# The front of a banded-attention and feed-forward kernel, planned by another rule for the port that VectorE and GpSimd share, with the weight casts on other engines

## The chip, the cores and the metric

The kernel runs on one core of a Trainium2 chip. The metric is the device time of one execution in microseconds (us), as the median of several executions. In the text PE or TensorE is the matrix engine, DVE is VectorE, ACT is ScalarE, POOL is GpSimd and SP is SyncE, which issues nearly all DMAs of this kernel.

## What is computed

Eight batches of eight heads with 576 positions of 64 elements go through attention within a window of 32 positions to either side. The result, read as 4608 tokens of 512 elements, goes through two matrix products with a squared ReLU between them:

```python
scores = scale * np.matmul(q, k.transpose(0, 1, 3, 2))
mask = np.abs(pos[:, None] - pos[None, :]) <= window          # window = 32
scores = np.where(mask, scores, -1000000000.0)
attn = np.exp(scores - np.max(scores, axis=-1, keepdims=True))
attn = attn / (np.sum(attn, axis=-1, keepdims=True) + 1e-09)
x = np.matmul(attn, v)            # then turned into (4608, 512)
...
h = x @ w_in                      # (4608, 512) @ (512, 2048)
r = np.maximum(h, 0.0)
g = s * (r * r) + b
return (g @ w_out).astype(np.float32)   # (4608, 2048) @ (2048, 512)
```

All inputs and the output are float32; the kernel computes its matrix products in bf16.

## The kernel before

The tokens are cut into 36 attention tiles of 128 (index `j`). Tiles 0 and 1 take a short way (`attend_light`): their scores are computed twice, plain and transposed, so that no transposition of the exponentials is needed. Their maxima are taken by DVE, split into two bf16 parts (`M16`, lines 861 and 863), turned on PE (`flip`, line 819), copied (`MT`), subtracted on PE (`less`, line 824), and ACT takes the exponential. Then come the product with V (`av`, lines 833 to 840), the division (`XN`, line 892), a turn back on PE (line 900) and a copy into `XT`, from which the feed-forward part reads. The other tiles go through `attend`: scores on PE (line 938), mask and maximum on DVE (line 950), exponential on ACT (line 958), the sum's reciprocal on DVE (line 967), the division of P (line 972), a transposition of P by PE (line 995, tiles below 5) or by DMA (line 986), and the product with V (line 1017 below tile 8, lines 1034 and 1040 from there on).

K and Q of the first 576 positions come in by four raw loads, `K0`, `K1`, `Q0` and `Q1`, one half of the heads each. They are cast to bf16 in pieces (`FLAT`), turned by PE (line 679) and copied into `TURN`. Tiles 0 to 3 read those. Later K and Q come in row order (`r32k`, `r32q`), are cast (`KQN`) and are turned by PE (line 756) or, above tile 11, by DMA.

The feed-forward part works on tiles of tokens, `TILES`, 8 of 128 and then 14 of 256. For each it multiplies by `WIN` in groups of 16 matmuls (8 of twice the width in a wide tile; line 1170), ACT applies the ReLU (line 1179), DVE squares into `GT` (line 1198), and PE multiplies `GT` by `WOUT`, in four parts of four matmuls, one part for each quarter of `w_out` (line 1220). The first scale and bias come in through `cvec` and `spread_scalars`: DVE splits `s` and `b` into three bf16 parts (lines 1087 and 1090), PE spreads them over the partitions.

`w_in` and `w_out` are loaded as float32 in four quarters each (`i0` to `i3`, `o0` to `o3`; line 584) into staging slots (`SLOT`), which lie in parts of `GT` that are not in use yet, and in the output buffers (slot 4). Each quarter is cast to bf16 by four casts (`cast`, through `move`, whose DVE and POOL form is line 633 and whose ACT form is line 638). `WSET` names the engines that may do that.

The order of the instructions on every engine is fixed when the program is built, by the planner `_Plan`. Each operation is a node with a key, an engine or a tuple of engines to choose from, a cost in ns for each, and what it reads and writes. `order` goes through time: it takes the engine that is free first, and there the ready node with the lowest key. With a choice of engines, a node is left to another engine if it would end sooner there. Every engine then runs its list in that order, and semaphores hold an instruction until what it needs is done; nothing else orders the engines. Where PE stands idle in the plan, `fill` writes in matmuls on constants (lines 555 and 559). `FIRST` gives the order of the first loads on SP's queue, `LEAD`, `L0` and `LS` by how many tokens attention's keys run ahead of those of the feed-forward part (`akey`), `RELU`, `AVK`, `HC`, `HT_`, `CB`, `SKEY` and others shift the keys of single operations, and `HOLD` is by how much a key may be higher for PE to stay with small matmuls. `CSET` names the engines for the casts of K and Q, `FLEX` those for the copies of turned K and Q, `NDIV` the tiles below which DVE may divide P, `NSQ` those in which POOL may square.

Of the kernel before, what the change touches and what calls it, by code (L numbers as in the profile page):

```python
# [11 lines left out]
S = 576  # L12
# [14 lines left out]
HOLD, DEFER, CHANGE = 200.0, 200.0, 97.0  # L27
LOOK, LOOK_GAP, LOOK_END = 0.0, 0.0, 400000.0
WARM, WARM_LOW, WARM_OVER, WARM_NS, WINDOW, WARM_END = 1.0, 0.66, 0.0, 225.0, 3413.0, 28000.0
BANKS_ = (("HT", 1), ("HT", 0), "AV", "TP")  # L30
FILL, FILL_MIN, FILL_SHARE, FILL_NS = ("attn", "sums"), 400.0, 0.5, 220.0


class _Node:
# [4 lines left out]
                 "hard", "mode", "ahead", "end")  # L39

    def __init__(self, nid, eng, fn, cost, lat, key, dsem, ndma, dtime):
        self.nid = nid
        self.eng = eng
        self.fn = fn
        self.cost = cost
        self.lat = lat
        self.key = key
        self.deps = {}
        self.dsem = dsem
        self.ndma = ndma  # L50
        self.dtime = dtime
# [11 lines left out]
        self.mode = "full"  # L63
        self.ahead = ()
        self.end = None
# [24 lines left out]
class _Plan:  # L90
# [11 lines left out]
    def add(self, eng, fn, cost, key, reads=(), writes=(), dsem=None, ndma=1, dtime=0.0,  # L102
# [3 lines left out]
        n.ndesc = ndesc  # L106

# [40 lines left out]
    def order(self):  # L148
# [5 lines left out]
        free = {e: START for e in self.ENGS}  # L154
        done = []
# [26 lines left out]
        while len(out) < len(self.nodes):  # L182
# [39 lines left out]
            if isinstance(n.eng, tuple):  # L222
                for x in n.eng:
                    cand[x].remove(n)
                n.eng, n.cost, n.fn = e, n.cost[e], n.fn[e]
            else:
                cand[e].remove(n)
            out.append(n)
# [132 lines left out]
def bass_sliding_window_symmetric__then__act_starrelu_kernel(  # L361
# [13 lines left out]
    TILES = [128] * 8 + [256] * 14  # L375
    assert sum(TILES) == T
    LEAD, L0, LS = 560, 600, 70
    NSQ = 8
    RELU, SQ = 900, 200
    FIRST = "Q0 K0 Q1 K1 i0 v0 v1 i1 i2|v2 i3 k2 o0 v3 q4 q5 v4 o1 o2 o3||v5||"  # L380
    ANY = ("act", "dve", "pool")
    WSET = {"i": ("pool", "act", "dve"), "o": ("act", "pool", "dve")}
    VOP = 12
    HSTEP, CB, VOK = 1.5, -400, -100
    NFLEX, TAIL = 10, 2
    PDMA, KQDMA, AHEAD, GATE = 5, 11, 4, 5
    CKEY, SKEY = 100, -300
    SLOT = dict(i0=0, i1=1, i2=2, i3=3, o0=0, o1=1, o2=4, o3=2)
    RAWNS, NSPLIT = 1450, 1
    HC, HT_ = -500, 150  # L390
    WHOLE, LIGHT, CH, NDIV = 4, 2, S // 16, 2
# [5 lines left out]
    AVK, NOLD, ONE, NVO, DA = 384, 8, 11, 2, 2  # L397
# [5 lines left out]
    def CSET(j):  # L403
        return ("pool",) if j >= 8 else ("pool", "act")
# [7 lines left out]
    with ExitStack() as es:  # L412
# [672 lines left out]
        def spread_scalars(x1):  # L1085
            for i in range(3):
                add("dve", lambda e, i=i: e.tensor_copy(SC3[:, i, :], SC1[:, i, :]), 100, SKEY,
                    reads=["SC1"], writes=[("SC3", i)], after=[x1])
                if i < 2:
                    add("dve", lambda e, i=i: e.tensor_tensor(  # L1090
                        SC1[:, i + 1, :], SC1[:, i, :], SC3[:, i, :], ALU.subtract), 100, SKEY,
                        reads=["SC1", ("SC3", i)], writes=["SC1"])

            def spread_sc(e):
                for i in range(3):
                    r = e.matmul(TPF[:, 0:2], lhsT=ONES[0:1, 0:128], rhs=SC3[:, i, :], start=(i == 0),
                                 stop=(i == 2))
                return r

            add("pe", spread_sc, 200, SKEY, reads=["ONES"] + [("SC3", i) for i in range(3)], writes=["TP"])  # L1100
# [15 lines left out]
        def attention_until(n):  # L1116
            if n and done[0] == 0:
                loads(0)
            for j in range(done[0], n):
# [13 lines left out]
                if j == 1:  # L1133
                    spread_scalars(lastx[0])
# [166 lines left out]
```

## Time and profile before

| what | value |
|---|---|
| median of 3 runs | 317.06 us (316.82 to 317.52) |
| the profiled execution's own time | 316.83 us |
| its span, first to last instruction | 315.1 us |
| PE busy | 302.9 us, 96% of the span |
| DVE busy | 226.0 us, 72% |
| ACT busy | 229.6 us, 73% |
| POOL busy | 149.6 us, 47% |
| granted TensorE clock | 1.000 |

The span is what lies between the first and the last instruction; the rest of the time lies around it. Busy shares are means over the whole span, so that a stretch of 20 us in which another engine is full can't be seen in them: it takes the view of busy time by windows, and the timeline of the engine in question. In a timeline row stand start and length in us, the engine, the line, the operation, what is written and read, the shapes, the count, and in brackets the idle time before it and what ended that. A few per cent of the matmul records are missing, and a missing one shows as idle time of PE.

### The profile page before, as it was taken

What the parts mean: (1) busy time and instruction counts of PE and PEld (TensorE: products, weight loads), DVE (VectorE), ACT (ScalarE), POOL (GpSimd) and SP (SyncE); (2) the same over time, 40 slices, a digit from 0 to 9 for tenths busy, and PEclk for the clock granted to TensorE, in tenths of its full rate; (3) what the DMA queues carried; (4) which work ended last, traced back from release to release, by engine and by line L of the source; (5) the groups of instructions that cost most, each with busy time, mean ns of one, the idle gap of its engine ahead of it and who ended that gap; (6) DMA issues with size and microseconds to landing.
All of it is one profiled execution on the core that took longest, in us unless ns stands there. A gap on an engine that the chain in (4) does not pass through costs nothing.

```text
span 315.1 us, 10310 instructions
## 1 busy us (share of the span) xinstructions
PE 302.9 (96%) x4006; PEld 210.6 (67%) x4054; DVE 226.0 (72%) x915; ACT 229.6 (73%) x763; POOL 149.6 (47%) x195
## 2 busy tenths in 40 slices
PE   7998989999999999999999999999999999999996
PEld 3567757677776666677676666666766666676574
DVE  5779998978887867587787677767776766773343
ACT  6559767898678969597879687868787787873240
POOL 5435555377564746646454545554564555130000
PEclk9999999999999999999999999999999999999999
DMA  7999999899999999999999999799999872432101
GB/s 289 351 342 244 292 301 215 232 155 210 211 209 222 199 209 225 228 213 174 228 239 178 182 215 260 159 233 175 249 177 251 145 162 68 69 69 67 69 34 69
DMA packets 156070, 61.57 MB, mean 195 GB/s; under 512 B 130164, under 2 KB 146932, under 8 KB 156020
## 3 DMA queue, kind: packets, MB, share of 16 engines
q1 hardware_dynamic: 156016, 60.90, 94.5%
q8 instruction: 32, 0.52, 0.7%
q14 instruction: 18, 0.15, 0.2%
q10 hardware_dynamic: 4, 0.00, 0.0%
HBM read 37.03 MB, written 9.44 MB: 147 GB/s over the span
## 4 chain that ended last, share of the span: by engine, by line
PE 88%; DVE 6%; issue 2%; DMA 2%; POOL 1%; SPq 0%; ACT 0%
PE ht L1170 37%; PE outp L1220 19%; PE ptp L1220 18%; PE sc L938 4%; DMA gt<-in_q_dram 2%; PE tp L1034 1%; PE av L1040 1%; DVE gt L1198 1%; PE sc L1220 1%; DVE ss L950 1%; PE tp L756 1%; POOL p L972 1%; DVE outs L1234 1%; PE ht L679 1%; DVE vo L633 1%
## 5 line engine op out<-in xcount | busy, mean ns | idle before, releaser
L1170 PE MATMUL ht<-xt,win 128*128 128x256 bf16 (+1 forms) x1408 | 146.4, 253 | 1.1 <-issue 1.0
L1170 PEld LDWEIGHTS ht<-xt,win 128*128 128x128 bf16 x1408 | 116.4, 98 | 32.1 <-issue 1.1
L958 ACT ACTIVATE p<-ss,mx 128x128 bf16<-128x128 f32 x272 | 113.4, 420 | 7.7 <-DVE mx L950 7.0
L1179 ACT ACTIVATE r<-ht 128x512 bf16<-128x512 f32 x144 | 84.6, 587 | 46.4 <-PE ht L1170 45.1
L1198 DVE TENSOR_TENSOR gt<-r 128x512 bf16<-128x512 bf16 x144 | 80.6, 560 | 48.3 <-ACT r L1179 46.5
L972 POOL TENSOR_TENSOR p<-p,rc 128x512 bf16<-128x512 bf16 x68 | 75.6, 1132 | 80.3 <-DVE rc L967 79.1
L1220 PE MATMUL outp<-wout,gt 128*128 128x512 bf16 (+1 forms) x263 | 68.0, 373 | 3.0 <-issue 1.5
L950 DVE CUSTOM_DVE_ANT_0 ss<-sc,mask 128x128 f32<-128x128 f32 x272 | 64.6, 280 | 7.8 <-PE sc L938 7.8
L1220 PE MATMUL ptp<-wout,gt 128*128 128x512 bf16 x251 | 65.0, 379 | 2.2 <-issue 1.6
L958 ACT ACTIVATION_READ_ACCUMULATOR p<-ss,mx 128x1 f32 x272 | 52.0, 191 | 0.0
L1220 PEld LDWEIGHTS outp<-wout,gt 128*128 128x128 bf16 x288 | 27.0, 98 | 19.6 <-issue 0.9
L1220 PEld LDWEIGHTS ptp<-wout,gt 128*128 128x128 bf16 x272 | 25.3, 98 | 21.2
L633 POOL CAST ve<-v 128x512 bf16<-128x512 f32 x37 | 23.8, 647 | 21.2 <-PE av L1040 19.4
L1049 ACT COPY half<-tp 128x512 f32<-128x512 f32 x28 | 16.4, 584 | 14.1 <-PE av L1040 13.8
L633 POOL CAST kn<-r32k 128x512 bf16<-128x512 f32 x31 | 19.8, 664 | 9.9 <-DMA r32k<-in_k_dram 9.8
L1051 DVE TENSOR_TENSOR xt<-av,half 128x512 bf16<-128x512 f32 x28 | 19.1, 682 | 4.5 <-ACT half L1049 4.4
L633 POOL CAST qn<-r32q 128x512 bf16<-128x512 f32 x30 | 20.0, 668 | 4.7 <-DMA r32q<-in_q_dram 4.7
L950 DVE DVE_READ_ACCUMULATOR2_ANT mx<- 128x1 f32 x272 | 21.4, 79 | 0.0
L938 PEld LDWEIGHTS sc<-kt,qt 64*64 64x64 bf16 x768 | 10.8, 108 | 8.9 <-issue 7.8
L964 DVE TENSOR_SCALAR sm<-sm 128x8 f32<-128x8 f32 x34 | 6.3, 184 | 12.5 <-ACT p L958 12.5
L938 PE MATMUL sc<-kt,qt 64*64 64x64 bf16 (+1 forms) x768 | 14.3, 204 | 0.0
L1234 DVE SCALAR_TENSOR_TENSOR outs<-outp,scb,cvec 128x512 f32<-128x512 f32 (+1 forms) x18 | 13.1, 726 | 1.1 <-PE outp L1220 0.9
(165 smaller groups left out, 220.0 us busy)
## 6 DMA issues: line engine op xcount, KB each, us to landing
out_dram<-outs SPq DMA_DIRECT2D x35, 256.0 KB, 3.1
v<-in_v_dram SPq DMA_DIRECT2D x28, 256.0 KB, 5.4
r32q<-in_q_dram SPq DMA_DIRECT2D x28, 256.0 KB, 4.6
r32k<-in_k_dram SPq DMA_DIRECT2D x9, 512.0 KB, 5.4
gt<-in_moe_w_in_dram SPq DMA_DIRECT2D x4, 1024.0 KB, 10.1
gt<-in_moe_w_out_dram SPq DMA_DIRECT2D x3, 1024.0 KB, 9.9
v<-in_v_dram SPq DMA_DIRECT2D x8, 192.0 KB, 4.7
r32k<-in_k_dram SPq DMA_DIRECT2D x3, 448.0 KB, 4.6
```

The costliest lines, as they stand in the source:

```text
L633: return e.tensor_copy(dst, src)
L938: r = e.matmul(SC[hh][64 * u:64 * u + 64, pr, x0:x1], lhsT=qq, rhs=kk, start=True, stop=True)
L950: lambda e, ss=ss, x=x, y=y, pr=pr, hh=hh: e.tensor_tensor_reduce(out=SS[ss][:, x, :], in0=SC[hh][:, pr, :], in1=MASK[kind][:, :], scale=- ...
L958: lambda e, ss=ss, x=x, y=y: e.activation(P[pb][:, y, :].rearrange("q (a p t) -> q a p t", a=2, t=2), spread(SS[ss][:, x, :]), AF.Exp, bia ...
L972: return e.tensor_tensor(P[pb][:, y0:y0 + 4, :], P[pb][:, y0:y0 + 4, :], RC[mb][:, y0:y0 + 4].unsqueeze(2).broadcast_to([128, 4, 128]), AL ...
L1049: add("act", lambda e: e.copy(HALF[hb][:, :], AV2[:, :]), 482, key + AVK, reads=[AV2N], writes=[("HALF", hb)])
L1051: add("dve", lambda e: e.tensor_tensor(XT[:, :, 128 * (j % NX):128 * (j % NX) + 128], AV[:, :, :], HALF[hb][:, :].rearrange("p (a b) -> p ...
L1170: r = e.matmul(hbank[:, nt * f:nt * f + nt], lhsT=WIN[:, kc, 128 * ft:128 * ft + 128], rhs=XT[:, kc, x0:x0 + nt], start=(kc == 0), stop=(k ...
L1179: return e.activation(R1[rb][:, :], hbank[:, :], AF.Relu, bias=0.0, scale=1.0)
L1198: return e.tensor_tensor(d, r, r, ALU.mult)
L1220: r = e.matmul(op_[:, 0:cn], lhsT=GT[:, g_, fc, :], rhs=WOUT[:, fc, c0:c0 + cn], start=(fc == 0), stop=(fc == 15))
L1234: add("dve", lambda e, ob=ob, op_=op_, c0=c0, cn=cn: e.scalar_tensor_tensor(OUTS[ob][:, 0:cn], op_[:, 0:cn], SCB[:, 0:1], CVEC[:, c0:c0 + cn],
```

## The change

The planner gets a rule for the port that DVE and POOL share. Every node that writes one of the named tensors (`SHARED`) is marked. When a POOL node, or a marked DVE node, is placed before 70 us of planned time, its cost is made longer by what the other engine's last such node still has to run, less 100 ns (DVE) or 140 ns (POOL). The rule acts in the planner's reckoning only: no instruction and no semaphore is added for it.

Beside it the parameters are set anew. `w_in`'s 16 casts may be done by POOL alone, `w_out`'s 16 by ACT or POOL, none by DVE. `FIRST` loads both halves of Q ahead of K, `q4` and `v3` ahead of `o0`, and `k2` behind it; the staging slots of `o1`, `o2` and `o3` change, so that `o3` now waits for `o0`'s casts. K and Q casts are for any engine below tile 4 and for POOL from there on. DVE may divide P below tile 6. ScalarE may copy turned K and Q below tile 4 only. The splitting of the scalars becomes a function of its own with an early key, ahead of all attention. Ten tiles of 128 tokens stand in front, and 13 of 256 behind them. `HOLD` is doubled, and the keys of attention's first tiles, of the ReLU and of the product with V move.

```diff
-HOLD, DEFER, CHANGE = 200.0, 200.0, 97.0
-LOOK, LOOK_GAP, LOOK_END = 0.0, 0.0, 400000.0
+HOLD, DEFER, CHANGE = 400.0, 200.0, 97.0
+LOOK, LOOK_GAP, LOOK_END = 0.0, 50.0, 400000.0
+HELD, HELD_END = {"dve": 100.0, "pool": 140.0}, 70000.0
+SHARED = ("FLAT", "WIN", "WOUT", "VE", "VO", "KQN", "GT", "M16", "SC1", "SC3")
...
+        if writes:
+            n.shared = (writes[0][0] if isinstance(writes[0], tuple) else writes[0]) in SHARED
...
+            n.base = n.cost
+            if (e == "pool" or e == "dve" and n.shared) and t < HELD_END:
+                n.cost += max(0.0, held["dve" if e == "pool" else "pool"] - t - HELD[e])
+                held[e] = t + n.cost
...
-    TILES = [128] * 8 + [256] * 14
+    TILES = [128] * 10 + [256] * 13
-    LEAD, L0, LS = 560, 600, 70
-    NSQ = 8
-    RELU, SQ = 900, 200
-    FIRST = "Q0 K0 Q1 K1 i0 v0 v1 i1 i2|v2 i3 k2 o0 v3 q4 q5 v4 o1 o2 o3||v5||"
+    LEAD, L0, LS = 560, 470, 40
+    NSQ = 0
+    RELU, SQ = 700, 200
+    FIRST = "Q0 Q1 K0 K1 i0 v0 v1 i1 i2 v2 i3 q4 v3 o0|k2 q5 v4 o1 o2 o3 v5||||"
-    WSET = {"i": ("pool", "act", "dve"), "o": ("act", "pool", "dve")}
-    VOP = 12
+    WSET = {"i": ("pool",), "o": ("act", "pool")}
+    VOP = 8
-    NFLEX, TAIL = 10, 2
+    NFLEX, TAIL = 4, 2
-    CKEY, SKEY = 100, -300
-    SLOT = dict(i0=0, i1=1, i2=2, i3=3, o0=0, o1=1, o2=4, o3=2)
+    CKEY, SKEY = 100, -9350
+    SPLIT1, SPKEY = True, -9000
+    SLOT = dict(i0=0, i1=1, i2=2, i3=3, o0=0, o1=4, o2=1, o3=0)
-    HC, HT_ = -500, 150
-    WHOLE, LIGHT, CH, NDIV = 4, 2, S // 16, 2
+    HC, HT_ = -9500, -50
+    WHOLE, LIGHT, CH, NDIV = 4, 2, S // 16, 6
-    AVK, NOLD, ONE, NVO, DA = 384, 8, 11, 2, 2
+    AVK, NOLD, ONE, NVO, DA = 320, 8, 11, 2, 2
-        return ("pool",) if j >= 8 else ("pool", "act")
+        return ("pool",) if j >= 4 else ANY
...
-        def spread_scalars(x1):
+        def split_scalars():
             for i in range(3):
-                add("dve", lambda e, i=i: e.tensor_copy(SC3[:, i, :], SC1[:, i, :]), 100, SKEY,
-                    reads=["SC1"], writes=[("SC3", i)], after=[x1])
+                add("dve", lambda e, i=i: e.tensor_copy(SC3[:, i, :], SC1[:, i, :]), 100, SPKEY,
+                    reads=["SC1"], writes=[("SC3", i)], after=[lastx[0]] if lastx[0] else [])
...
+        def spread_scalars():
             def spread_sc(e):
...
                 loads(0)
+                if SPLIT1:
+                    split_scalars()
...
-                    spread_scalars(lastx[0])
+                    if not SPLIT1:
+                        split_scalars()
+                    spread_scalars()
```

More of the change, by code (lines that the diff above doesn't have):

```diff
@@ L38 @@
                  "nout", "left", "ready", "users", "seq", "used", "val", "snap", "pre", "tag", "ndesc",
-                 "hard", "mode", "ahead", "end")
+                 "hard", "mode", "ahead", "end", "shared", "base")
     def __init__(self, nid, eng, fn, cost, lat, key, dsem, ndma, dtime):
@@ L63, in __init__ @@
         self.mode = "full"
+        self.shared = False
+        self.base = 0.0
         self.ahead = ()
@@ L154, in order @@
         free = {e: START for e in self.ENGS}
+        held = {"dve": 0.0, "pool": 0.0}
         done = []
@@ L1083, in cvec @@
                 reads=["TP", "SCB"], writes=["CVEC"])
-        def spread_scalars(x1):
+        def split_scalars():
             for i in range(3):
-                add("dve", lambda e, i=i: e.tensor_copy(SC3[:, i, :], SC1[:, i, :]), 100, SKEY,
-                    reads=["SC1"], writes=[("SC3", i)], after=[x1])
+                add("dve", lambda e, i=i: e.tensor_copy(SC3[:, i, :], SC1[:, i, :]), 100, SPKEY,
+                    reads=["SC1"], writes=[("SC3", i)], after=[lastx[0]] if lastx[0] else [])
                 if i < 2:
                     add("dve", lambda e, i=i: e.tensor_tensor(
-                        SC1[:, i + 1, :], SC1[:, i, :], SC3[:, i, :], ALU.subtract), 100, SKEY,
+                        SC1[:, i + 1, :], SC1[:, i, :], SC3[:, i, :], ALU.subtract), 100, SPKEY,
                         reads=["SC1", ("SC3", i)], writes=["SC1"])
+        def spread_scalars():
             def spread_sc(e):
@@ L1098, in spread_sc @@
                 return r
-            add("pe", spread_sc, 200, SKEY, reads=["ONES"] + [("SC3", i) for i in range(3)], writes=["TP"])
+            add("pe", spread_sc, 200, SKEY, reads=["ONES"] + [("SC3", i) for i in range(3)],
+                writes=["TP"])
             add("act", lambda e: e.copy(SCB[:, :], TPF[:, 0:2]), 250, SKEY, reads=["TP"], writes=["SCB"])
```

## The prediction

> **What bounds the kernel now.** I read the busy table of the page first, then busy time by windows, then the chain of waits between 23 and 45 us, then the timelines of DVE, POOL and PE there. All numbers are of the profiled execution (316.83 us, span 315.1). The windows, with engines in the order PE, weight load, DVE, ACT, POOL:
>
> ```profile
> core 0: us, PE busy (x) PEld busy (x) DVE busy (x) ACT busy (x) POOL busy (x), PEclk, DMA share, GB/s
> 5.00:23.00 18.00, 17.23 (x338) 10.44 (x338) 13.32 (x36) 10.28 (x24) 7.23 (x12) 1.00 1.09 360
> 23.00:45.00 22.00, 18.92 (x337) 15.74 (x340) 21.73 (x83) 17.00 (x56) 13.07 (x16) 1.00 1.03 285
> 45.00:70.00 25.00, 24.31 (x338) 17.03 (x341) 21.36 (x87) 21.40 (x75) 13.55 (x18) 1.00 1.03 198
> 70.00:300.00 230.00, 226.57 (x2894) 156.82 (x2933) 162.21 (x687) 174.47 (x599) 112.29 (x137) 1.00 0.99 182
> ```
>
> From 70 us on PE is full and DVE is at 70%: what comes after the front is matrix work that this change leaves as it is. Between 45 and 70 us PE lacks 0.69 us. The one stretch in which PE is not full and another engine is, is 23 to 45 us: DVE 21.73 of 22.00, PE 18.92, so 3.08 us without a PE record. (Part of that is missing records.) Between 5 and 23 us PE is busy 17.23 of 18.00, but the matmuls on constants that the planner writes into its idle time (line 555) are in it:
>
> ```profile
> 5.00:23.00 18.00, 4.28 (x14) 1.02 (x14) 1.00 1.09 360
> ```
>
> So 4.28 us of that stretch is filling. Reclaimable in the front are 4.28 + 0.77 (5 to 23 us), 3.08 and 0.69: under 8.9 us. The first 5 us belong to the first loads and don't change. The chain of waits (start, length, what) says who is responsible behind 24.9 us:
>
> ```profile
> 25.94 0.33 DVE xn L892
> 26.27 0.75 DVE win L633 x2
> ...
> 28.62 0.08 DVE sc L1087
> 28.70 0.19 DVE ss L950
> 28.89 0.01 DVE mx L950
> 28.89 0.07 DVE sc L1090
> 28.97 0.17 DVE sm L964
> 29.13 0.06 DVE sc L1087
> 29.19 0.18 DVE rc L967
> 29.37 0.01 DVE sc L1090
> ...
> 29.59 0.93 DVE sc L1087
> ...
> 32.03 0.06 DVE wout L633
> 32.09 0.61 issue
> 32.70 0.75 DVE wout L633 x2
> ...
> 38.27 2.63 POOL p L972 x2
> ...
> 40.95 0.62 PE av L995 x8
> ```
>
> The chain runs through DVE until 38.2 us, then through two divisions of P on POOL, and reaches PE only at 40.95.
>
> **What the change takes off that chain.** The rows just shown give the terms. `w_in`'s two casts: 0.75 us, gone from DVE. `w_out`'s three casts with the gap between them: 0.06 + 0.61 + 0.75 = 1.42 us, gone from DVE. The five scalar operations: 0.08 + 0.07 + 0.06 + 0.01 + 0.93 = 1.15 us, moved ahead of attention. Together 3.32 us. The 0.93 is a cast of two numbers; the next rows show why it took so long:
>
> ```profile
> 29.52 1.00 DVE L1087 CAST sc<-sc 1x2 bf16<-1x2 f32 x1
> ```
>
> ```profile
> 29.46 1.04 POOL L972 TENSOR_TENSOR p<-p,rc 128x512 bf16<-128x512 bf16 x1 [1.17 <-DVE sc L1090]
> ```
>
> It ended (30.52) with POOL's division (30.50). That is the shared port, which the old planner did not reckon with, and it also stretches the squares and casts beside POOL work. By engine, from 11.7 to 48.4 us (count, busy us, mean ns), DVE first, then POOL and ACT:
>
> ```profile
> L1198 DVE TENSOR_TENSOR gt<-r 128x512 bf16<-128x512 bf16 x12 | 7.2, 599 | 0.3
> ...
> L633 DVE CAST wout<-gt 128x512 bf16<-128x512 f32 x7 | 3.8, 594 | 0.0
> L633 DVE CAST win<-gt 128x512 bf16<-128x512 f32 x7 | 3.0, 470 | 0.5 <-DMA gt<-in_moe_w_in_dram 0.5
> ...
> L633 DVE CAST wout<-outs 128x512 bf16<-128x512 f32 x2 | 1.2, 618 | 0.0
> ```
>
> ```profile
> L633 POOL CAST win<-gt 128x512 bf16<-128x512 f32 x6 | 4.0, 687 | 10.0 <-DMA gt<-in_moe_w_in_dram 10.0
> ```
>
> ```profile
> L638 ACT CAST win<-gt 128x512 bf16<-128x512 f32 x3 | 1.8, 615 | 0.0
> ```
>
> In all DVE loses 3.8 + 3.0 + 1.2 = 8.0 us of casts. What comes back to DVE: divisions of P, now allowed to it for tiles 2 to 5, and casts of K and Q below tile 4. DVE shows no division of P; its nearest row is the square of the same shape (line 1198), 0.60 us. One such division and no cast would be 0.6, two of each (a cast at 0.47) 2.1, none at all 0; I take 0.8 us, near the single division.
>
> **What is late next.** A DVE chain shorter by 3.32 - 0.8 = 2.5 us can't move PE by more than its idle time, 3.08 us less the missing records. The other things due there are the transfers. POOL's waits for the last quarters of `w_in` and `w_out` end on landings:
>
> ```profile
> 25.05 1.36 POOL L633 CAST win<-gt 128x512 bf16<-128x512 f32 x2 [2.92 <-DMA gt<-in_moe_w_in_dram]
> 44.38 0.62 POOL L633 CAST wout<-gt 128x512 bf16<-128x512 f32 x1 [1.24 <-DMA gt<-in_moe_w_out_dram]
> ```
>
> The DMA share is over 1 in both stretches and the new `FIRST` moves the same bytes ahead of `i3` and of `o3`, so those landings stay near 25 and 44 us. The last group of the first feed-forward tile can't start before `i3` is cast: by POOL alone 4 x 0.69 = 2.7 us after landing (25.05 + 2.7 = 27.8), against 27.0 now (26.27 + 0.75 in the chain). The 0.8 us is covered by the groups of the second tile and by attention's matmuls; without that cover it costs 0.8. `o3` now waits in its slot for `o0`'s four casts; on SP's queue behind it stand `v5` and the later loads of q, k and v. I cost that at nothing, because `o0`'s casts stand at 32 us in the chain and the last landing of `w_out` at 44.4, 12 us later; if ACT leaves `o0`'s casts behind its exponentials, the whole queue slips with it, by the 0.62 of a cast for each of two. I therefore take 1.6 us of gain from this stretch, between 0 and 3.1.
>
> **Before 23 us.** `XT`'s first tile ends at 22.9, and PE's first feed-forward group follows at once:
>
> ```profile
> 22.33 0.59 ACT L638 COPY xt<-tp 128x512 bf16<-128x512 bf16 x1 [1.18 <-PE tp L900]
> ```
>
> ```profile
> 23.15 1.06 PE L1170 MATMUL ht<-xt,win 128*128 128x128 bf16 x16
> ```
>
> Loading Q whole first delays the first half of the heads by one load, but the second half of K now gets cast and turned as soon as it lands, and it is the second half that ends last. Five of DVE's seven `w_in` casts and all three of ACT's lie in this stretch beside the short attention; POOL, now busy 7.23 of 18 us, takes these eight and is then busy 7.2 + 8 x 0.69 = 12.7. Each holds the port. What that costs is seen once:
>
> ```profile
> 16.47 0.16 DVE L861 CAST m<-mx 128x4 bf16<-128x4 f32 x1
> ...
> 17.59 0.60 DVE L861 CAST m<-mx 128x4 bf16<-128x4 f32 x1
> ```
>
> ```profile
> 17.56 0.61 POOL L633 CAST win<-gt 128x512 bf16<-128x512 f32 x1 [2.80 <-DMA gt<-in_moe_w_in_dram]
> ```
>
> The same small cast takes 0.16 us alone and 0.60 beside a `w_in` cast: 0.44 us. Eight such operations (lines 861 and 863, four half tiles) lie on the chain to the first two `XT` tiles. I take one in seven of them as newly hit, 0.5 us, between 0 and 8 x 0.44 = 3.5. The Trainium skill ("SBUF — State Buffer", section "Who interferes with whom") says that the pair of ports is held for a whole instruction and that the second to come fully blocks; by that rule eight casts more could cost DVE up to 8 x 0.69 = 5.5 us, an estimate from POOL's row, and the sum would come out 3.3 us above the time now instead of below it. The two rows agree with the rule for one meeting; how many meet, only the new order decides. Against this I set 0.8 us of filling saved of the 4.28, between -1 and 2.5.
>
> **Two more narrow tiles** cost PE a little:
>
> ```profile
> 47.76 0.89 PE ht L1170 x16
> ...
> 99.83 0.87 PE ht L1170 x8
> ```
>
> Eight groups more at 0.89 instead of 0.87: +0.16 us. `NSQ` and `LOOK_GAP` change nothing: POOL squares nothing in this trace, and `LOOK` is 0. `HOLD`, `RELU` and `AVK` reach past the front, where PE lacks 3.4 of 230 us: nothing, give or take 0.5.
>
> **Sum.** -1.6 (23 to 45 us) - 0.8 (before 23) + 0.5 (port) + 0.16 (tiles) = -1.74 us: 316.83 becomes 315.1 in a profiled execution. The median of the runs is 0.23 above the profiled one, so 315.3 for the median. A measurement of this kernel can tell about 0.2% from no change, 0.63 us.
>
> **Rivals.**
> - *GpSimd holds the port against the short attention* (slower). It decides if more than half of the eight small operations, or the `w_in` casts themselves, come late: 6 x 0.44 = 2.6 us on `XT`'s first tile, of which the gains before 23 us return 0.8, and nothing is won behind it because the DVE chain starts later by as much: 317.06 + 2.6 - 0.8 = 318.9; with four hit, 318.0. For it: POOL's 12.7 busy us in that stretch, against 7.2. Against: the planner now reckons with such meetings and shifts its order by them. Chance 0.28.
> - *The transfers set the pace anyway* (same). DVE is relieved, but PE meets `i3` at 25 and `o3` at 44 us with nothing else ready, and idle time only moves: 317.06 + 0.16 = 317.2. For it: a DMA share of 1.03 to 1.09. Against: the chain of waits holds DVE and not a transfer from 25 to 38 us. That the new rule changes nothing on the chip, since it adds no wait and only reorders, comes out here too. Chance 0.14.
> - *The whole chain comes off.* DVE gives 2.5 us, and POOL's two divisions at 38.27 (2.63 us) go to DVE for 1.2, another 1.4, of which PE's idle time lets 3.1 through; with 1 us of filling saved: 317.06 - 4.1 + 0.16 = 313.1. Chance 0.18.
>
> **How the numbers follow.** The forecast, 315.3, has 0.40 (its own range is 314.0 to 316.4); with the last rival and the near edge of the others this makes 0.58 for faster by over 0.2%, 0.14 for within 0.2%, 0.28 for slower. The range reaches from somewhat below the last rival, 312.6, to somewhat under the first one's full price, 318.5; beyond it remain the hits of six or more and a gain of more than all idle time.
>
> **What would show it.** In the new trace: DVE busy below 20 of 22 us and PE above 20 between 23 and 45; no `sc` row at line 1087 longer than 0.2 us; matmuls of line 555 under 3.5 us; the first row of line 1170 at about 22.3 us; from 70 us to the end no change beyond 0.5 us. It is wrong if the first group of line 1170 starts behind 23.2 us with rows of line 861 at 0.4 us or more ahead of it, or if DVE is relieved and PE still lacks 3 us while waiting for casts of `win` or `wout`.

## The result and the profile after

The changed kernel takes 315.44 us (median of 6 runs, 314.54 to 316.29) against 317.47 us of the kernel before (median of 6): a ratio of 0.9936, 95% interval 0.9914 to 0.9958. Measured again twice with more runs it took 316.2 us (0.9963, interval 0.9946 to 0.9980) and 316.1 us (0.9958, interval 0.9932 to 0.9985). So the change gains 1.1 to 2.0 us, 0.4 to 0.6%. The profiled execution is the slowest of its six, 316.29 us with a span of 314.4; the profiled one of before had 316.83 and 315.1. Their difference is therefore smaller than that of the medians. Two runs of *casts alone*, two of *casts back* and one of the kernel before with less output, all told of below, had a granted clock of 0.97 to 0.99 and were up to 8 us longer; the medians leave them out.

Busy time by windows of the kernel after, in the stretches of the prediction (PE, weight load, DVE, ACT, POOL; then granted clock, DMA share, GB/s):

```profile
core 0: us, PE busy (x) PEld busy (x) DVE busy (x) ACT busy (x) POOL busy (x), PEclk, DMA share, GB/s
5.00:23.00 18.00, 17.60 (x330) 10.45 (x332) 12.08 (x35) 9.57 (x23) 9.97 (x17) 1.00 1.10 361
23.00:45.00 22.00, 21.27 (x384) 17.56 (x383) 20.94 (x83) 20.25 (x64) 14.74 (x20) 1.00 1.09 294
45.00:70.00 25.00, 24.47 (x369) 17.09 (x374) 22.11 (x81) 19.84 (x70) 16.52 (x23) 1.00 0.97 215
70.00:300.00 230.00, 225.76 (x2918) 158.02 (x2956) 163.15 (x686) 174.09 (x596) 113.32 (x135) 1.00 0.99 180
```

Between 23 and 45 us PE is busy 21.27 us instead of 18.92, and DVE, which had 21.73 of 22 us, still has 20.94. From 70 to 300 us PE has 225.76 us where it had 226.57: 0.8 us more of idle time in a stretch that the change was not to touch. (Missing records count as idle in both sums, 3.1 us of "issue" before and 2.3 after over the whole execution, so that the real difference is larger; the lead, below, says two us.)

Where the gain of the front is can be read from PE's timeline between 23 and 46 us, from the rows that have idle time before them (in brackets, with what ended it). Before:

```profile
27.68 1.52 PE L1170 MATMUL ht<-xt,win 128*128 128x128 bf16 x24 [0.16 <-ACT r L1179]
30.15 1.50 PE L1170 MATMUL ht<-xt,win 128*128 128x128 bf16 x24 [0.95 <-issue]
33.73 0.81 PE L1220 MATMUL outp<-wout,gt 128*128 128x512 bf16 x3 [0.48 <-DVE wout L633]
35.18 0.32 PE L1017 MATMUL av<-pts,ve 128*64 128x64 bf16 x8 [0.19 <-DVE pts L633]
40.95 0.62 PE L995 MATMUL av<-ident,p 128*128 128x128 bf16 x8 [0.77 <-POOL p L972]
42.99 0.81 PE L1220 MATMUL outp<-wout,gt 128*128 128x512 bf16 x3 [0.53 <-issue]
```

After:

```profile
31.37 0.62 PE L1007 MATMUL av<-ident,p 128*128 128x128 bf16 x8 [0.26 <-POOL p L984]
34.31 0.81 PE L1238 MATMUL outp<-wout,gt 128*128 128x512 bf16 x3 [0.16 <-issue]
40.54 0.81 PE L1238 MATMUL outp<-wout,gt 128*128 128x512 bf16 x3 [0.16 <-issue]
41.50 0.32 PE L1029 MATMUL av<-pts,ve 128*64 128x64 bf16 x8 [0.15 <-DVE pts L645]
```

The gaps before sum to 3.08 us, those after to 0.73. (The `x3` with "issue" are groups of four of which one record is missing, so a little of both sums is no wait.) The waits for DVE's `wout` cast (0.48), for POOL's division (0.77) and for the third group of the first feed-forward tile (0.95) are gone or smaller.

To follow the lead over the whole execution I count PE's main matmul groups in both traces (feed-forward, scores, product with V, the turns of K and Q, and the spread scales), each with the same duration per kind, and compare how much of that work has been started at the same moment. The kernel after is 0.2 us behind at 23 us, 2.5 ahead at 45, 2.8 at 70, 2.4 at 150, 1.6 at 200, 0.8 at 220 and 0.7 at the end, which is the difference of the two spans. (With other durations per kind the leads of this document move by up to 0.7 us; read them as that good.) A row that stands in both traces shows the same: the sixteen matmuls that spread the scales start at 48.58 us before and at 46.35 after.

```profile
48.58 1.05 PE L1065 MATMUL tp<-wout,ones 128*32 128x512 bf16 x16
```

```profile
46.35 1.05 PE L1077 MATMUL tp<-wout,ones 128*32 128x512 bf16 x16
```

So the front wins 2.5 to 2.8 us, and in this execution two of them are given back in the middle. What takes them is named in the view of PE's waits (line, releaser, total, times, longest) and, with start and length, in the chain of waits:

```profile
PE tp L1046 <- DMA pts<-p: 1.1, 3, 0.5
```

```profile
159.75 6.50 DMA pts<-p
...
205.76 6.59 DMA pts<-p
```

These are transpositions of P by DMA, for which the first product with V of a tile waits; its three waits are at 134.6, 165.9 and 211.9 us. The kernel before has none of the kind. From 125 to 221 us the thirteen transpositions of P land 0.2 us later in the mean than before (the twelfth, for one, at 143.09 us before and 143.51 after), though PE is some 2 us further. In the kernel before, each lands 0.7 us or more ahead of the first product with V that uses it. In the kernel after, six between 130 and 215 us land only 0.04 us ahead of it: PE had been waiting for them.

### The profile page after: what moved, and what is told of

The parts are those of the page before. It is cut to its first block, busy times and chain, and to the rows that moved or that the text cites. A ratio compares the mean times of both kernels' runs of the same rounds, so it can differ in the third digit from the quotient of the medians.

```text
span 314.4 us, 10451 instructions
## 1 busy us (share of the span) xinstructions
PE 304.5 (97%) x4074; PEld 212.4 (68%) x4123; DVE 224.7 (71%) x903; ACT 228.9 (73%) x762; POOL 158.1 (50%) x208
## 4 chain that ended last, share of the span: by engine, by line
PE 70%; DVE 9%; DMA 8%; ACT 5%; SPq 3%; POOL 2%; issue 2%; DVEq 0%
PE ht L1188 28%; PE outp L1238 15%; PE ptp L1238 14%; DMA pts<-p 6%; DVE gt L1216 3%; PE sc L950 2%; ACT p L970 2%; POOL p L984 2%; DVE ss L962 2%; SPq L625 2%; DMA r32q<-in_q_dram 1%; PE tp L1046 1%; ACT r L1197 1%; PE sc L1238 1%; PE tp L768 1%
## 5 line engine op out<-in xcount | busy, mean ns | idle before, releaser
L1188 PEld LDWEIGHTS ht<-xt,win 128*128 128x128 bf16 x1472 | 118.0, 98 | 31.3 <-DVE xt L1063 0.2
L1216 DVE TENSOR_TENSOR gt<-r 128x512 bf16<-128x512 bf16 x144 | 82.0, 571 | 50.3 <-ACT r L1197 49.2
L984 POOL TENSOR_TENSOR p<-p,rc 128x512 bf16<-128x512 bf16 x64 | 71.9, 1141 | 57.0 <-DVE rc L979 57.0
L645 POOL CAST kn<-r32k 128x512 bf16<-128x512 f32 x33 | 21.4, 675 | 25.4 <-DMA r32k<-in_k_dram 25.4
L645 POOL CAST ve<-v 128x512 bf16<-128x512 f32 x37 | 24.1, 652 | 19.5 <-PE av L1052 12.9
L645 POOL CAST qn<-r32q 128x512 bf16<-128x512 f32 x32 | 22.8, 714 | 7.9 <-DMA r32q<-in_q_dram 7.8
L976 DVE TENSOR_SCALAR sm<-sm 128x8 f32<-128x8 f32 x34 | 7.1, 208 | 12.4 <-ACT p L970 12.4
```

The costliest lines, as they stand in the source:

```text
L645: return e.tensor_copy(dst, src)
L984: return e.tensor_tensor(P[pb][:, y0:y0 + 4, :], P[pb][:, y0:y0 + 4, :], RC[mb][:, y0:y0 + 4].unsqueeze(2).broadcast_to([128, 4, 128]), AL ...
L1188: r = e.matmul(hbank[:, nt * f:nt * f + nt], lhsT=WIN[:, kc, 128 * ft:128 * ft + 128], rhs=XT[:, kc, x0:x0 + nt], start=(kc == 0), stop=(k ...
L1216: return e.tensor_tensor(d, r, r, ALU.mult)
```

## The experiments

### The same program again: is the lead lost in every execution?

The changed kernel went with two other series, unchanged.

> The changed kernel itself, beside the three others on one chip. Its first six executions took 314.5 to 316.3 us; expected 315.4 us here, 2.0 below the kernel before. Its first profile had PE 2.5 to 2.8 us ahead of the kernel before at 70 us and 0.7 us ahead at the end. If the transfers give that lead back (theory), the profile here again has TensorE waiting for transposed P (pts) between 120 and 220 us, over 1 us in sum; if the first profile was an accident of one execution, no such waits.

> The changed kernel again, as the base for the three beside it: 315.4 to 316.2 us, 1.2 to 2.0 below the kernel before. If the lead is won in the front and given back in the middle in every execution, its profile has PE at 21 of 22 us or more between 23 and 45 us, and a lead over the kernel before that is at least 1 us smaller at 220 us than at 70.

Measured: 316.2 us and 316.1 us, as told above. The profiled executions differ more than the medians do. In the first repetition it is its slowest (317.98 us, span 316.1), in the second one of its faster ones (315.07 us, span 313.2). Busy time between 170 and 220 us, and in the first PE's wait beside it; in the second there is none of that kind:

```profile
170.00:220.00 50.00, 48.36 (x592) 32.81 (x590) 34.87 (x153) 38.62 (x137) 24.85 (x30) 1.00 1.13 202
...
PE tp L1046 <- DMA pts<-p: 2.3, 4, 1.3
```

```profile
170.00:220.00 50.00, 50.00 (x606) 34.04 (x605) 36.29 (x151) 38.88 (x137) 26.54 (x32) 1.00 1.16 212
```

Three executions of one program: the front gains 2.6, 2.8 and 3.0 us by 70 us (first repetition, first profile, second repetition); PE then waits 2.3, 1.1 and 0 us for `pts`, the lead at 220 us is -0.7, 0.8 and 1.8 us, and the spans are 316.1, 314.4 and 313.2. So the first repetition has the waits that I expected, and the second has none: its lead falls by over 1 us too, but for another reason.

PE works in the same order in all three, so that they can be laid side by side, group by group. At 131 us the first profile is 0.8 us ahead of the second repetition, and at 222 us 1.2 us behind it. These 2.0 us are lost at the six products with V named above and nowhere else (the view of waits lists 1.1 of them). The first repetition loses 3.1 us against the second between 131 and 231 us, in the same way. The second itself loses 0.9 us against the first profile at 80 us, where PE waits for a cast of Q (`PE tp L768 <- POOL qn L645: 0.7, 1, 0.7`). So what the middle takes back is late transpositions of P, and how many are late differs from one execution to the next. Why one lands late in one execution and not in another these traces don't show.

### Casts and rule, one at a time

My theory was that the casts that leave DVE make the gain and that the rule for the port only orders; its rival was that the rule carries it. Four kernels: the casts alone put into the kernel before, the casts taken back out of the kernel after, the rule switched off in the kernel after, and the rule alone in the kernel before.

```diff
# kernel before, casts alone
-    WSET = {"i": ("pool", "act", "dve"), "o": ("act", "pool", "dve")}
+    WSET = {"i": ("pool",), "o": ("act", "pool")}
# kernel after, casts back: the same two lines the other way round
# kernel after, no turns
-HELD, HELD_END = {"dve": 100.0, "pool": 140.0}, 70000.0
+HELD, HELD_END = {"dve": 100.0, "pool": 140.0}, 0.0
# kernel before, rule alone: HELD, HELD_END, SHARED, n.shared and the
# lines on n.cost and held[e] as in the change, all parameters as before
```

> The kernel before, with the weight casts alone moved (w_in to GpSimd, w_out to ScalarE and GpSimd). Theory, the DVE chain from 25 to 38 us ends TensorE's idle time and the casts are most of what is taken off it: PE busy 20.0 to 20.8 of 22 us between 23 and 45 us (18.9 before), and 1.0 to 1.5 us less time than before. Rival, the planner's new reckoning with the shared port is what gains, and without it the casts on GpSimd meet VectorE where nobody planned it: same time as before or up to 1 us more, with DVE rows of lines 861 and 863 longer than 0.4 us ahead of the first feed-forward group.

> The changed kernel, with the weight casts given back to the engines that had them before; everything else new, the planner's rule too. Theory: DVE is full again between 23 and 45 us, and the time is 1.0 to 1.8 us above the changed kernel. Rival (the rule gains): within 0.5 us of the changed kernel.

> The changed kernel, with the planner's rule for the shared port switched off (HELD_END 0), so that the same parameters are planned by the old reckoning. Theory (the casts gain, the rule only orders): 0 to 0.6 us above the changed kernel. Rival (the rule gains): 1.2 to 2 us above it, near the kernel before.

> The kernel before with the planner's rule for the shared port alone; parameters, casts and loads as before. Theory (rule and new casts gain only together, since with the casts on VectorE it stays full): within 0.6 us of the kernel before, DVE above 21 of 22 us between 23 and 45 us. Rival (the rule itself gains): 1.2 to 2 us below it.

| kernel | us | ratio to before, interval | lead over before at 45 / 70 / 220 us |
|---|---|---|---|
| casts alone | 316.92 | 0.9986, 0.9972 to 0.9999 | 1.3 / -0.3 / -0.4 |
| casts back | 317.10 | 0.9998, 0.9980 to 1.0016 | 1.8 / 1.1 / 0.8 |
| no turns | 317.61 | 1.0021, 1.0000 to 1.0041 | -0.1 / -0.3 / -0.7 |
| rule alone | 319.91 | 1.0087, 1.0068 to 1.0107 | about +0.2 until 50 us, -0.2 at 90, -3 from 150 on |

My theory fell: without the rule nothing of the gain is left (1.4 us above the changed kernel, 0.8 more than the theory allowed), and the casts alone bring 0.4 us where I expected 1.0 to 1.5. The rival met its forecast in *no turns* and missed it in the others: *casts back* is 0.9 us above the changed kernel and not within 0.5, so that almost nothing is left without the casts either, and *rule alone* is 2.8 us slower than before and not faster. The window from 23 to 45 us, in the order of the table:

```profile
23.00:45.00 22.00, 21.51 (x364) 17.00 (x352) 19.12 (x83) 20.01 (x65) 14.39 (x20) 1.00 1.00 282
```

```profile
23.00:45.00 22.00, 21.61 (x377) 16.94 (x376) 20.87 (x85) 18.83 (x63) 10.44 (x14) 1.00 1.11 287
45.00:70.00 25.00, 24.55 (x371) 17.05 (x373) 24.54 (x85) 18.93 (x69) 15.56 (x20) 1.00 1.02 210
```

```profile
23.00:45.00 22.00, 20.59 (x373) 16.80 (x374) 20.68 (x84) 17.19 (x56) 13.65 (x19) 1.00 1.07 283
```

```profile
23.00:45.00 22.00, 20.48 (x343) 15.99 (x341) 19.79 (x81) 20.46 (x68) 11.84 (x15) 1.00 1.00 275
...
70.00:120.00 50.00, 48.09 (x739) 33.10 (x736) 38.87 (x169) 39.84 (x146) 31.31 (x39) 1.00 1.06 208
```

With the casts alone DVE falls to 19.12 us, further than with the whole change, and PE is 1.3 us ahead at 45 us. ACT, which now has half of `w_out`, then brings K and Q too late, and one wait takes the lead back at 55 to 60 us:

```profile
PE tp L756 <- ACT qn L638: 1.2, 1, 1.2
```

With the casts back on DVE the front wins 1.8 us, but DVE has 24.54 of 25 us behind it, and 0.7 us are lost there. Without the rule the program starts its first feed-forward group at 24.88 us instead of 23.25 and waits 1.3 us once for a copy of P on DVE. With the rule alone the front is level with before, and my expectations (DVE above 21 us, a time within 0.6 us of before) were wrong; the loss lies behind 90 us, where the new order has `PE tp L1045 <- DVE xt L1062: 1.6, 1, 1.6` among its waits.

What has to be kept in mind with all of these: each edit makes the planner order everything anew, so that a kernel differs from its neighbour in more than the named part. One such difference can be counted: in the changed kernel PE does the small matmuls of scores and of the product with V side by side 26 times between 70 and 300 us, in *casts back* and *no turns* 23 times. At the price of about 0.23 us each that is worked out further below, up to 0.7 us of what these two lose comes from there. So the four kernels show that neither part brings the gain alone in these orders. They don't price each part.

### Less output written

If transfers take the lead back, fewer transfers should leave it. Here both kernels write 64 columns of every output tile except those of the last rows, which leaves out most of the output write and no arithmetic; the order on every engine stays.

```diff
-                        e.dma_start(out[r0:r0 + 128, c0:c0 + cn], OUTS[ob][:, 0:cn])],
+                        e.dma_start(out[r0:r0 + 128, c0:c0 + (cn if r0 + 128 == T else 64)], OUTS[ob][:, 0:(cn if r0 + 128 == T else 64)])],
```

> The kernel before with 64 of 512 columns of each output tile written, the last tile whole (most of the output is left out); the order of all instructions is the same. It takes some 8 of 61 MB off the DMA engines. Theory, in the changed kernel the transfers in the middle give TensorE's lead back, while in the kernel before they just keep up: 0 to 0.7 us below the kernel before. Rival, the give-back has nothing to do with the transfers: this and the next fall by the same.

> The changed kernel with 64 of 512 columns of each output tile written, the last tile whole (most of the output is left out); the order of all instructions is the same. Theory (transfers give the lead back): 1.0 to 2.0 us below the changed kernel's 315.4 to 316.2, TensorE waiting for pts under 0.5 us, and a lead over the kernel before of over 1.8 us left at 220 us. Rival (something else in the order): falls by no more than the kernel before does, and the lead still goes.

Measured: the kernel before stays where it was, 317.33 us (1.0003, interval 0.9990 to 1.0016). The kernel after falls to 314.56 us (0.9921, interval 0.9895 to 0.9947). The window from 170 to 220 us, first of the kernel before and then of the one after, each with less output (between 120 and 170 us PE is full as well):

```profile
170.00:220.00 50.00, 50.00 (x603) 33.60 (x601) 36.24 (x159) 39.04 (x139) 25.30 (x32) 1.00 1.01 170
```

```profile
170.00:220.00 50.00, 50.00 (x607) 34.06 (x606) 36.19 (x155) 39.65 (x140) 26.01 (x32) 1.00 1.05 174
```

No `pts` wait is left, and the lead of the one over the other is 1.4 us at 65 us, 2.0 at 150, 2.1 at 220 and 1.8 at the end: kept, not lost. Between the medians lie 2.8 us. The kernel before is not held up by its output.

That fits the transfers as the cause of the late transpositions, but it doesn't show it. The second repetition above kept its lead behind 81 us with the whole output written, so that one execution without these waits proves little. PE is 0.8 to 1.0 us later here than there from 81 us on, which alone gives the transpositions more time. And the interval of the ratio (0.9895 to 0.9947) overlaps the one of the first measurement of the changed kernel (0.9914 to 0.9958). Which transfer would be the tight one (the writes themselves, or the loads and transpositions queued with them) these two runs don't tell either.

The front won less in this execution although its order is that of the changed kernel: the first feed-forward group starts at 24.49 us and not at 23.24 as in the second repetition. A matmul on constants takes 0.39 us there from 6 us on, and here still 0.61 us until 8.5 us, with a granted clock of 1.00 in both.

### Planning the transposition of P later

If PE waits for `pts`, the planner can be told that this DMA lands 1.5 us later, and will put other work ahead of the product with V.

```diff
-                end = dma_free[e] + (LAND if early else 700.0)
+                end = dma_free[e] + (LAND if early else 700.0 + 1500.0 * n.dsem.startswith("dpt"))
```

> The changed kernel, where the planner, behind 60 us of its time, reckons 1.5 us more until a transposition of P by DMA has landed. That puts the product with V one or two groups of matmuls later on TensorE, behind the same scores. Theory (the lead is lost in waits for pts): those waits under 0.5 us, and 0.7 to 1.5 us below the changed kernel. Rival (the transfers set the rate whatever TensorE does first, or a later product with V costs more changes between small and full matmuls, 0.11 us each): no faster than the changed kernel, up to 2 us slower.

Measured: 316.68 us (0.9984, interval 0.9959 to 1.0009), no better, as the rival said. Two things come together. First, the front wins less in the profiled execution, though the order of every engine is that of the changed kernel up to 43 us: `o0` lands at 32.9 us and not at 29.6, ACT stands idle for it (`32.92 0.62 ACT L650 CAST wout<-gt 128x512 bf16<-128x512 f32 x1 [1.78 <-DMA gt<-in_moe_w_out_dram]`), and PE waits 0.92 us at 34 us for the ReLU behind that cast. So the front's gain hangs on transfers as well. Second, the waits for `pts` are gone and PE is at 50.00 of 50 us in every window from 70 to 220 us, but the lead melts from 0.8 us at 70 us to -0.3 at 220 all the same. PE is full and does less: the planner no longer puts the scores of one tile and the product with V of another next to each other. In the changed kernel 26 stretches between 70 and 300 us hold both and 3 hold one; here 20 hold both and 15 one. The price of that is seen better in the next experiment.

### Three edits of the changed kernel: scalars late, divisions on POOL, eight narrow tiles

```diff
# scalars late
-    CKEY, SKEY = 100, -9350
-    SPLIT1, SPKEY = True, -9000
+    CKEY, SKEY = 100, -300
+    SPLIT1, SPKEY = False, -300
# divisions on POOL
-    WHOLE, LIGHT, CH, NDIV = 4, 2, S // 16, 6
+    WHOLE, LIGHT, CH, NDIV = 4, 2, S // 16, 2
# eight narrow tiles
-    TILES = [128] * 10 + [256] * 13
+    TILES = [128] * 8 + [256] * 14
```

> The changed kernel with the five scalar operations back behind the second tile, with their key of before. Theory (the prediction's term): they stand in the DVE chain again, about 28 to 30 us, for 0.3 to 1.15 us, by whether POOL holds the port at that moment: 0.3 to 1.0 us above the changed kernel. Rival: DVE has idle time there now, so that they cost nothing: within 0.3 us.

> The changed kernel with all divisions of P on GpSimd again (NDIV 2). Theory: of the two divisions of a tile one on each engine ends 1 us sooner than both on POOL, and PE waits for P at the front (rows of lines 984 and 1007 between 29 and 41 us); without it 0.5 to 1.3 us above the changed kernel. Rival: DVE, freed of its share of the divisions (0.67 us and more each), gives that back: within 0.4 us.

> The changed kernel with 8 tiles of 128 and 14 of 256 tokens, as before the change. The prediction's price for two more narrow tiles was 0.16 us, so 0.16 us less here. Theory: no more than that, 0 to 0.4 us below the changed kernel, the front being the same program up to the ninth tile. Rival: ten narrow tiles feed PE better while attention runs behind; 0.5 us or more above it.

They went with the second repetition of the changed kernel (316.1 us, before 317.27).

*Scalars late*: 316.86 us (0.9977, interval 0.9960 to 0.9994), 0.8 above the changed kernel as I expected, but the intervals overlap, so that the time alone doesn't tell them apart. The lead is 1.6 us at 45 us and 1.2 at 70, against 2.6 and 3.0. The small operations are back between 28.6 and 31.8 us, and the last two, right behind a division of P, are long:

```profile
29.30 1.48 DVE L984 TENSOR_TENSOR p<-p,rc 128x512 bf16<-128x512 bf16 x1
30.70 0.56 DVE L1102 TENSOR_TENSOR sc<-sc,sc 1x2 f32<-1x2 f32 x1
31.40 0.43 DVE L1099 CAST sc<-sc 1x2 bf16<-1x2 f32 x1
```

But PE is level with the changed kernel until 36 us. What it loses in the front, it loses behind that, mostly in two waits that the changed kernel doesn't have at that place:

```profile
36.69 0.61 PE L768 MATMUL tp<-ident,qn 128*128 128x128 bf16 x8 [0.45 <-ACT kt L650]
40.96 0.62 PE L1007 MATMUL av<-ident,p 128*128 128x128 bf16 x8 [0.50 <-DVE p L984]
```

One is for a copy of turned K by ACT, the other for a division of P that the new order puts on DVE. So a front with the scalars late is worse, but not by the time of the scalars themselves.

*Divisions on POOL*: 316.5 us (0.9972, interval 0.9951 to 0.9994). With 0.4 us above, and intervals that overlap, no difference can be told. The profile says that none is to be expected in the front: with all four divisions on POOL PE is busier there than in the changed kernel, and its lead is 3.0 us at 45 and at 70 us.

```profile
23.00:45.00 22.00, 21.95 (x387) 17.47 (x379) 19.80 (x79) 20.61 (x64) 15.12 (x22) 1.00 1.10 293
```

So no gain from the permission for DVE to divide can be seen. (This kernel also has 22 joined stretches instead of 26 behind 70 us, 0.9 us at the price worked out below, so that the run doesn't price the permission by itself.)

*Eight narrow tiles*: 319.62 us (1.0078, interval 1.0050 to 1.0107), 3.5 us above the changed kernel where I expected it a little below; the rival's number was met, but the rows below give another reason than the rival's. The front is as before the edit (lead 2.5 us at 45, 2.8 at 70); the loss comes between 100 and 260 us, where PE is still called full but does less. Rows of PE's timeline, first of the repetition of the changed kernel, then of this one (start and length):

```profile
204.02 1.03 PE L1238 MATMUL outp<-wout,gt 128*128 128x512 bf16 x4
204.98 0.41 PE L950 MATMUL sc<-kt,qt 64*64 64x128 bf16 x22
...
205.60 1.92 PE L1188 MATMUL ht<-xt,win 128*128 128x256 bf16 x16
```

```profile
194.74 0.24 PE L1046 MATMUL tp<-pts,ve 64*64 64x128 bf16 x2
...
195.11 1.04 PE L1238 MATMUL ptp<-wout,gt 128*128 128x512 bf16 x4
...
196.95 0.45 PE L950 MATMUL sc<-kt,qt 64*64 64x128 bf16 x24
197.33 1.05 PE L1188 MATMUL ht<-xt,win 128*128 128x256 bf16 x8
```

Scores and product with V side by side go through PE together in 205.60 - 204.98 = 0.62 us; apart they take 197.33 - 196.95 = 0.38 and 195.11 - 194.74 = 0.37. And each change from the large matmuls to the small costs about 0.1 us more: four `outp` matmuls take 0.86 us from start to start among their like, but 0.96 (204.02 to 204.98) in front of scores. The Trainium skill ("TensorEngine Tiling (Array Packing)", section "Key Properties") has such a change of mode drain TensorE; it gives no price, and these rows agree with it at about 0.1 us. A pair that is split thus costs 0.38 + 0.37 + 0.10 - 0.62 = 0.23 us. The changed kernel has 26 joined stretches between 70 and 300 us, this one 12: 14 x 0.23 = 3.2 us, against 3.5 between the medians and 4.8 between these two spans. That is worked out, not tried by itself. What two narrow tiles themselves cost can't be seen beside it.

No kernel of these is faster than the changed one with its whole output written.

## Why the prediction was right, and where its steps were not

The time came as forecast (315.3 against 315.44, 316.2 and 316.1), and so did the reason, as far as kernels that are each planned anew can show it: DVE's chain between 23 and 45 us was the bound, and lightening it with the port reckoned in feeds PE. The loads, keys and tiles that were set beside it were mostly not tried one by one. But that the sum came out is in part luck: errors in both directions met, and the measured gain itself was 2.0, 1.1 and 1.2 us against the 1.7 forecast.

**23 to 45 us, forecast -1.6.** PE's idle time there fell from 3.08 to 0.73 us, its lead at 45 us is 2.5 us. The term was too small by about one us. (What I called a gap of 0.61 us between the three casts of `w_out` is in DVE's timeline the first cast itself, 0.83 us long; the sum stays.) I had taken the middle of 0 to 3.1. DVE did not fall below 20 us of 22, as I had said it would, but only from 21.73 to 20.94. In this window 4.7 us of weight casts and 1.5 us of scalar operations are gone from it. What came in their place is in part work that the lead brought forward (twelve squares and not nine, one copy more into `XT`), in part casts of V and K, and two divisions at 2.2 us, more than the 0.8 that I had given back for all that returns:

```profile
L984 DVE TENSOR_TENSOR p<-p,rc 128x512 bf16<-128x512 bf16 x2 | 2.2, 1102 | 0.0
```

So what counted was less how busy DVE is than in which order it works, and the run without the rule fits that: DVE 20.68 us there, less than here, and PE 0.7 us worse, with no lead at all. That the rule "adds no wait and only reorders" stood in the rival of no change; without that reordering the gain was gone. (Up to 0.7 us of that run's loss lies in the joined stretches, as said.)

**The landings** stayed near 25 and 44 us as said, and even came earlier:

```profile
24.25 2.48 POOL L645 CAST win<-gt 128x512 bf16<-128x512 f32 x4 [1.54 <-DMA gt<-in_moe_w_in_dram]
...
43.22 1.36 POOL L645 CAST wout<-gt 128x512 bf16<-128x512 f32 x2 [1.90 <-DMA gt<-in_moe_w_out_dram]
```

`i3`'s casts, by POOL alone, end at 26.7 us, not at 27.8, because `i3` landed 0.8 us earlier and four casts behind each other took 2.48 us and not 2.7. The new wait of `o3` cost nothing, as said: no row of PE waits for `wout`.

**The scalars, 1.15 us of the chain.** They now run at 4 to 6 us, as said. What that earns is not shown: with them back the front's lead is 1.0 us smaller at 45 us, but by two waits elsewhere, and the time differs by 0.8 us with overlapping intervals.

**Before 23 us, forecast -0.8.** Wrong. The first feed-forward group starts at 23.25 us instead of 23.15, and the filling grew from 4.28 to 5.45 us:

```profile
23.25 1.07 PE L1188 MATMUL ht<-xt,win 128*128 128x128 bf16 x16
```

```profile
5.00:23.00 18.00, 5.45 (x18) 1.00 1.10 361
```

**The port before 23 us, forecast +0.5.** Mis-sized. I took one in seven of the eight small operations as newly hit; five of the eight are at 0.5 us or more, where before it was one:

```profile
12.36 0.56 DVE L873 CAST m<-mx 128x4 bf16<-128x4 f32 x1
12.96 0.51 DVE L875 TENSOR_TENSOR m<-mx,m 128x4 bf16<-128x4 f32 x1
16.27 0.17 DVE L873 CAST m<-mx 128x4 bf16<-128x4 f32 x1
17.41 0.58 DVE L875 TENSOR_TENSOR m<-mx,m 128x4 bf16<-128x4 f32 x1
18.00 0.56 DVE L873 CAST m<-mx 128x4 bf16<-128x4 f32 x1
...
21.09 0.51 DVE L875 TENSOR_TENSOR m<-mx,m 128x4 bf16<-128x4 f32 x1
```

```profile
11.72 2.29 POOL L645 CAST win<-gt 128x512 bf16<-128x512 f32 x4 [2.32 <-DMA gt<-in_moe_w_in_dram]
...
17.36 2.29 POOL L645 CAST win<-gt 128x512 bf16<-128x512 f32 x4 [1.62 <-DMA gt<-in_moe_w_in_dram]
19.86 2.29 POOL L645 CAST win<-gt 128x512 bf16<-128x512 f32 x4 [0.21 <-DMA gt<-in_moe_w_in_dram]
```

Each hit lies inside a `w_in` cast of POOL. All eight took 1.83 us before and take 3.46 now: 1.63 us more, over three times my term. The Trainium skill ("SBUF — State Buffer", section "Who interferes with whom") has the port held for a whole instruction; the rows agree, since the hit operation lasts about as long as one cast, at most 0.58 us, whatever its own 0.17. So the first rival's condition was met, over half of the eight hit, and also what I had named as proof of error, a first group behind 23.2 us with such rows ahead of it. Its price didn't come: the first group is 0.1 us late and not 2.6 less 0.8. That fits DVE's other work there, which fell (13.32 to 12.08 us busy with the hits in it), and the new order of the loads of K and Q; no run tried which. And the rival's "nothing is won behind it" was wrong as well.

**Two narrow tiles, forecast +0.16.** The price of the tile itself may be right, but it is not what the parameter does. Taking the two tiles away costs 3.5 us, and 3.2 of that can be worked out from the order of the small matmuls that comes with it.

**From 70 us on, forecast nothing, give or take 0.5.** Wrong, and the largest error. In the profiled execution the lead of 2.8 us at 70 us is 0.7 at the end; in the second and the first repetition the spans differ from before's by -1.9 and +1.0. Late transpositions of P account for the 2.0 us that the first profile loses against the second repetition. I had read "PE is full there" as "a lead is passed on". The trace of before has no wait of PE for a transposition anywhere, and I took that for slack without asking how much: the shortest time there between a landing and the use of it is 0.7 us (100.17 and 100.88 us), the next 0.9 (213.03 and 213.92). A PE that is 2.8 us earlier gets there ahead of some of them. The second rival said of the front that the transfers set the pace anyway; it holds, in part, for the middle, where I had not looked, and for the front of one execution, where `o0` came late.

## What to carry to other kernels

A stretch in which the bound engine is full passes a lead on only if nothing else there is as tight: before counting a gain of the front to the end, ask how long before its use each transfer of the middle lands, and take the smallest of these slacks as the lead that is safe. With a planner, every parameter is a new order for the whole program; a part's price can be read from its own rows, but its effect on the time only from the windows, and a worse time after an edit may come from a place that the edit doesn't name. An engine at full busy time can still do less work per us. Two executions of one program work in the same order, so that laying them side by side group by group shows exactly where time is lost. And two engines that share a port can want a suitable order as much as a smaller load: here neither alone brought the gain.

## What the runs showed of the hardware

- A DVE operation on 128 x 4 elements takes 0.17 us alone and 0.51 to 0.58 us beside a cast of 128 x 512 on GpSimd; one on 1 x 2 elements 0.15 us alone, 0.43 and 0.56 right behind a division in the run with the scalars late, and 1.00 in the kernel before.
- Small matmuls of two kinds (24 of scores, and the product with V) run through PE in 0.62 us when they are mixed and in 0.75 when they are apart, and a change from large to small matmuls costs about 0.1 us more.
- The transposition of P by DMA lands 3.8 us behind its issue in the median of the kernel before and 4.4 in that of the changed kernel (the row below), and took 6.5 and 6.6 us where PE waited for it:

```profile
pts<-p SPq DMA_TRANSPOSE x31, 4.4
```

- One program's spans, with the granted clock at 1.00 each time, lay between 313.2 and 316.1 us in three profiled executions, and the leads of the front were alike in all three. In the run with less output, whose order is the same, PE's matmuls on constants (128 x 512) took 0.61 us each until 8.5 us, where in these three they had come down to 0.39 by 6.2 us, and the first feed-forward group started 1.2 us later.
